# The last token group of the last projection: one sum formed in PSUM ahead of its product, two blocks stored by accumulation

## Chip, cores and metric

One core of one Trainium2 chip. The metric is the device time of one execution in microseconds (us), the median over several executions. "Span" is the length of the profiled execution, some 2 us shorter than the measured time. In the text PE is the matmul engine (TensorE), DVE is VectorE, ACT is ScalarE, POOL is GpSimd, SP is SyncE, which here only issues transfers. PSUM is the on-chip memory that the matmuls write to, SBUF the on-chip memory of all other tiles. A transfer lands when its completion is signalled; "landing" is the time from its issue to that.

## The reference, cut to what matters

The program normalizes x (2048 tokens x 1024), computes a windowed attention s with an output projection wo, and a gated MLP g on the same normalized x, and returns x + s * g. All arrays are bf16.

```python
xn = _layernorm(x, axis=-1)
s = _A_ref(xn, A_wqkv, A_wo)          # ends with  @ wo
g = _silu(_B_ref(xn, B_w1, B_w3, B_w2))
return x + s * g
```

The end of the kernel is the projection `@ wo` for the last group of 512 tokens, times g, plus x.

## The kernel before

The projection works on 2 x 2 blocks with seven products in place of eight (Strassen-Winograd). A token group gives four output blocks of 256 KB, named (u, dh): u selects the half of the tokens, dh the half of the columns. `finished` takes a block out of PSUM, multiplies by g and stores it. The code is cut; tile allocations are left out.

```python
def wo(b):                                    # b == 1, gp == 1 is the last group
    ...
    for gp in G2:
        last = b == 1 and gp == 1
        product(both(pa), gp, a11, b11, True)
        product(both(pe), gp, s1, t1, True)
        flush()                               # last product of the group before
        # pb gets a copy of pa (ACT); in the last group, two tiles and two half copies
        act_copy(sp5[:], pe[:])
        product(pbs, gp, s2, t2, False)
        # su2 gets a copy of pb (ACT); in the last group, two half copies
        product(both(pe), gp, s4, b22, False)
        finished(b, 0, 1, gp, pe, su2[:])     # pe + su2, a sum on DVE
        product(pbs, gp, s3, t3, False)
        finished(b, 1, 1, gp, pb, sp5[:])     # pb + sp5, a sum on DVE
        product(both(pa), gp, a12, b21, False)
        finished(b, 0, 0, gp, pa)
        # tail, run later: product(pbs, gp, a22, t4, False); finished(b, 1, 0, gp, pb)

def finished(b, u, dh, gp, ps, add=None):
    ...
    if b == 0 or gp == 0:                     # x lies in the output already
        to_bf16(d, ps, add)
        anchor["v"] = nc.vector.tensor_mul(g, d, g)
        nc.gpsimd.dma_start(out=rows_, in_=g, accum_op=ALU.add)
    elif (u, dh) != (1, 0):                   # last group: x is added on DVE
        to_bf16(d, ps, add)
        nc.vector.tensor_mul(g, d, g)
        nc.vector.tensor_add(g, g, xw[u, dh])
        nc.sync.dma_start(out=rows_, in_=g)
    else:
        # block (1, 0) in two halves, each with its own store on SP
        ...
```

So in all groups but the last the block is added to x inside the transfer: x was copied to the output long before (`residual`), and POOL issues an accumulating store. In the last group x comes in through `xw`, and SP issues plain stores.

Of the kernel before, what the change touches and what calls it, by code (L numbers as in the profile page):

```python
# [9 lines left out]
BF16 = mybir.dt.bfloat16  # L10
# [7 lines left out]
def kernel(  # L18
# [11 lines left out]
    nc = tc.nc  # L30
# [5 lines left out]
    CH = 512  # L36
# [9 lines left out]
    I = range(2)  # L46
    scale = float(Dh) ** -0.5
    hp = tc.high_priority

    x_flat = A_x.rearrange("b s d -> (b s) d")  # L50
# [32 lines left out]
        out=ident[:], in_=ident[:], compare_op=ALU.not_equal, fill=1.0,  # L83
# [5 lines left out]
        out=ones4[:], in_=ones4[:], compare_op=ALU.is_ge, fill=0.0,  # L89
# [3 lines left out]
        out=ones4[:], in_=ones4[:], compare_op=ALU.is_ge, fill=0.0,  # L93
# [5 lines left out]
        out=maskb[0:32], in_=maskb[0:32], compare_op=ALU.is_ge, fill=-1.0e9,  # L99
# [11 lines left out]
    pb = keep.tile([P, W, P], BF16, name="pb")  # L111
# [16 lines left out]
    def rows(f0, n, dt=BF16):  # L128
        v = h_sb[:, f0:f0 + n, :].rearrange("p f n -> p (f n)")
        return v if dt is BF16 else v.bitcast(dt)  # L130

    def bank2(name):
        return psum.tile([P, 2, CH], FP32, tag="mm", name=name)

    def k4(name, shape=(2, CH), dt=FP32):
        return kk.tile([P, *shape], dt, tag="k4", name=name)
# [10 lines left out]
    def mm(ps, lhs, rhs, first):  # L147
        n = len(lhs)
        for k in range(n):
            with behind("pe") if "open" in anchor else nullcontext():  # L150
                anchor["pe"] = nc.tensor.matmul(  # L151
                    ps, lhsT=lhs[k], rhs=rhs[k], start=(first and k == 0),
                    stop=(k == n - 1), skip_group_check=not first,
                )
# [4 lines left out]
    def act_copy(out_, in_):  # L159
        with hp():  # L160
            nc.scalar.copy(out=out_, in_=in_)  # L161
# [3 lines left out]
    def flush():  # L165
        while pend:
            pend.pop(0)()
# [59 lines left out]
    def behind(key):  # L227
        return tc.issue_after(anchor[key].ins) if key in anchor else nullcontext()
# [162 lines left out]
    def att_tile(shape, dt, name):  # L391
        return att.tile([P, *shape], dt, tag="a8", name=name)
# [109 lines left out]
    def run_hooks():  # L502
        while hooks:
            hooks.pop(0)()
# [43 lines left out]
    def bg(us):  # L548
        if us <= 0:
            return  # L550
        state_p[0] = tc.cur_priority
        pace["credit"] += us - pace["owed"]
        pace["owed"] = 0
        with priority(BG), behind("v"):
            while pace["credit"] > 0:
                t = next(att_it)
                if t is STOP:
                    pace["credit"] = min(pace["credit"], 6)
                    break
                else:  # L560
                    pace["credit"] -= t
# [23 lines left out]
    def release(key):  # L585
        free.extend(held.pop(key, []))
# [158 lines left out]
    def g_tile(b, u, dh, gp):  # L745
        f0 = {(0, 0): 10, (1, 1): 10, (0, 1): 6, (1, 0): 6}[u, dh] + 2 * gp
        col = {(0, 0): 0, (1, 1): CH, (0, 1): 0, (1, 0): CH}[u, dh]
        return h_sb[:, f0:f0 + 2, col:col + CH]
# [109 lines left out]
    wx = {}  # L858
# [23 lines left out]
    def wo(b):  # L882
        (a11, a12, a21, a22, s1, s2, s3, s4), (b11, b12, b21, b22, t1, t2, t3, t4) = wx[b]
        if b == 1:
            xt4 = att_tile((2, 2, 2, CH), BF16, "xw")
            for u in I:
                for dh in I:
                    xw[u, dh] = xt4[:, u, dh]
                    with behind("dl"):
                        nc.sync.dma_start(out=xw[u, dh], in_=out_rows(x_flat, 1, u, dh, 1))  # L890

        def product(ps, gp, lhs, rhs, first):
            for i in I:
                g = gp * 2 + i
                mm(ps[i], [lhs[:, j, g * P:(g + 1) * P] for j in range(4)], [rhs[:, j, :] for j in range(4)], first)

        both = lambda t: [t[:, i] for i in I]
        for gp in G2:
            run_hooks()
            last = b == 1 and gp == 1  # L900
            pa = bank2(f"wa{b}_{gp}")
            product(both(pa), gp, a11, b11, True)
            pe = bank2(f"we{b}_{gp}")
            product(both(pe), gp, s1, t1, True)
            flush()
            pb = [bank2(f"wb{b}_{gp}{i}")[:, i] for i in I] if last else bank2(f"wb{b}_{gp}")
            for i in I:
                if last:
                    act_copy(pb[i], pa[:, i])
            if not last:  # L910
                act_copy(pb[:], pa[:])
            pbs = pb if last else both(pb)
            sp5, su2 = k4(f"wsp{b}_{gp}"), k4(f"wsu{b}_{gp}")
            act_copy(sp5[:], pe[:])
            bg((7, 0)[gp] * (1 - b))
            product(pbs, gp, s2, t2, False)
            for i in I:
                if last:
                    act_copy(su2[:, i], pb[i])
            if not last:  # L920
                act_copy(su2[:], pb[:])
            product(both(pe), gp, s4, b22, False)
            finished(b, 0, 1, gp, pe, su2[:])
            product(pbs, gp, s3, t3, False)
            finished(b, 1, 1, gp, pb, sp5[:])
            product(both(pa), gp, a12, b21, False)
            finished(b, 0, 0, gp, pa)

            def tail(gp=gp, pb=pb, pbs=pbs):
                product(pbs, gp, a22, t4, False)  # L930
                finished(b, 1, 0, gp, pb)

            pend.append(tail)
        flush()
        release("wo")

    def out_rows(ap, b, u, dh, gp):
        g0 = ((2 * b + u) * NST + gp * 2) * P
        return ap[g0:g0 + 2 * P, dh * CH:(dh + 1) * CH].rearrange("(i p) n -> p i n", p=P)

    def to_bf16(d, ps, add):
        if add is None:
            nc.scalar.copy(out=d, in_=ps[:])
        elif isinstance(ps, list):
            for i in I:
                nc.vector.tensor_add(d[:, i], ps[i], add[:, i])
        else:
            nc.vector.tensor_add(d, ps[:], add)

    xw = {}  # L950

    copies = [((2 * b + u) * CH, CH // (1 + b), dh) for b in I for u, dh in ((0, 0), (1, 1), (0, 1), (1, 0))]

    def residual():
        if copies:
# [4 lines left out]
    def finished(b, u, dh, gp, ps, add=None):  # L960
        g = g_tile(b, u, dh, gp)
        n = {(0, 0): 0, (1, 1): 2, (0, 1): 4, (1, 0): 0}[u, dh] + gp
        d = h_sb[:, 16 + 2 * n:18 + 2 * n, CH:]
        rows_ = out_rows(out_flat, b, u, dh, gp)
        with hp():
            if b == 0 or gp == 0:
                to_bf16(d, ps, add)
                anchor["v"] = nc.vector.tensor_mul(g, d, g)
                nc.gpsimd.dma_start(out=rows_, in_=g, accum_op=ALU.add)
            elif (u, dh) != (1, 0):  # L970
                to_bf16(d, ps, add)
                nc.vector.tensor_mul(g, d, g)
                nc.vector.tensor_add(g, g, xw[u, dh])
                nc.sync.dma_start(out=rows_, in_=g)
            else:
                for i in I:
                    if i == 0:
                        nc.scalar.copy(out=d[:, i], in_=ps[i])
                    nc.vector.tensor_mul(g[:, i], ps[i] if i else d[:, i], g[:, i])
                    nc.vector.tensor_add(g[:, i], g[:, i], xw[u, dh][:, i])  # L980
                    nc.sync.dma_start(out=rows_[:, i], in_=g[:, i])


# [126 lines left out]
    b12 = rows(12, 2).rearrange("p (k n) -> p k n", k=KH)  # L1110
# [134 lines left out]
    with behind("dl"):  # L1245
        nc.sync.dma_start(out=xT[:], in_=x_dram[:])
        nc.sync.dma_start(out=xs[:], in_=xs_dram[:])
    wo(0)
    state.add("wo")
    mlp_up(1)  # L1250
    mlp_down(1, lambda: mid(1), (7, 10, 10, 9, 9, 3))
    wo(1)


# [28 lines left out]
```

## Time and profile before

| | before |
|---|---|
| time, median (first 3 runs) | 724.18 us (723.66 to 724.26) |
| span of the profile | 721.8 us |
| PE's last matmul ends | 715.89 |
| last DVE instruction ends | 718.69, 2.80 past PE |
| span ends | 5.91 past PE |

The prediction below shows the busy table, the chain and the end in order of time. Who waited for whom in the last 22 us (engine, line, waited for: us in total, times, longest us):

```profile
DVE h_sb L948 <- ACT wsu L161: 2.0, 1, 2.0
...
ACT wsu L161 <- PE wb L151: 1.1, 1, 1.1
```

and the same for the DMA queue of SP over the end. The closing wait of the program on its stores:

```profile
SPq L1278 <- DMA out_dram<-h_sb: 1.1, 3, 0.5
```

The view is what the change attacks: DVE idles 2.0 us for the copy wsu, and then runs behind PE to the end.

### The profile page before, as it was taken

The numbers are of one execution on the slowest core, as the hardware profiler recorded it, in microseconds if no ns is written. First come the engines' busy times: TensorE is split into PE (matmuls) and PEld (weight loads), VectorE is DVE, ScalarE is ACT, GpSimd is POOL, SyncE is SP. The second block draws the span as 40 slices with busy tenths as digits, with TensorE's granted clock in tenths as the row PEclk, the third lists the DMA queues.
The fourth block names the chain that finished last, engine by engine and source line by source line (L and its number), as shares of the span: only waits on it lengthen the run. The fifth ranks groups of instructions, "written<-read, shape, count | busy, mean of one in ns | idle before, by whom it ended". The sixth has DMA issues, their size and how long they took to land.

```text
span 721.8 us, 8746 instructions
## 1 busy us (share of the span) xinstructions
PE 710.0 (98%) x3313; PEld 346.2 (48%) x3367; DVE 624.9 (87%) x690; ACT 312.9 (43%) x326; POOL 95.7 (13%) x162
## 2 busy tenths in 40 slices
PE   8999999999999999999999999999999999999996
PEld 6655565654444444444444444444444444444442
DVE  7996879779879878978999999969859989999974
ACT  5745334356545456555555312034364573020233
POOL 0011100012300000233111000000435004000011
PEclk9999999999999999999999999999999999999999
DMA  9946257777754523558756547469799444563615
GB/s 337 275 125 182 82 185 228 258 249 238 246 172 153 191 71 117 173 191 268 246 174 216 190 132 250 144 205 385 168 276 336 139 138 150 168 202 129 199 36 108
DMA packets 119193, 139.51 MB, mean 193 GB/s; under 512 B 17648, under 2 KB 94448, under 8 KB 118512
## 3 DMA queue, kind: packets, MB, share of 16 engines
q1 hardware_dynamic: 104608, 97.01, 42.6%
q0 software_dynamic: 14544, 41.95, 18.0%
q8 instruction: 26, 0.43, 0.2%
q14 instruction: 15, 0.12, 0.1%
HBM read 96.21 MB, written 38.80 MB: 187 GB/s over the span
## 4 chain that ended last, share of the span: by engine, by line
PE 95%; ACT 2%; DVE 2%; issue 1%; DMA 0%; DVEq 0%; ACTq 0%
PE bm L151 20%; PE am L151 13%; PE em L151 13%; PE db L151 10%; PE bq L151 9%; PE de L151 7%; PE da L151 7%; PE eq L151 5%; PE aq L151 3%; PE wb L151 2%; PE af L151 2%; PE we L151 2%; PE wa L151 2%; DVE h_sb L236 1%; PE af L1049 1%
## 5 line engine op out<-in xcount | busy, mean ns | idle before, releaser
L151 PEld LDWEIGHTS <-wring 128*128 128x128 f16 (+1 forms) x1792 | 183.4, 102 | 204.3 <-issue 2.2
L151 PEld LDWEIGHTS <-h_sb 128*128 128x128 f16 (+1 forms) x1056 | 109.5, 104 | 118.4 <-issue 0.6
L151 PE MATMUL bm<-xs,wring 128*128 128x512 f16 x504 | 117.4, 379 | 0.2
L151 PE MATMUL am<-xT,wring 128*128 128x512 bf16 x322 | 79.0, 379 | 0.8
L151 PE MATMUL db<-wring,h_sb 128*128 128x512 f16 x336 | 73.2, 379 | 0.0
L481 DVE TENSOR_TENSOR BC<-Ep,vT 128x2048 bf16<-128x2048 bf16 x56 | 66.6, 1217 | 0.1
L426 DVE TENSOR_TENSOR pt<-qt,kT 128x4096 bf16<-128x4096 bf16 x24 | 54.9, 2290 | 0.6
L664 DVE TENSOR_TENSOR um<-em,um 128x1024 f32<-128x1024 f32 x28 | 34.2, 1222 | 21.0 <-PE em L151 13.3
L666 ACT ACTIVATE g<-um 128x1024 bf16<-128x1024 f32 x28 | 29.6, 1057 | 48.6 <-DVE um L664 48.6
L151 PE MATMUL da<-wring,h_sb 128*128 128x512 bf16 x219 | 48.7, 379 | 0.3
L467 POOL DMA_DIRECT2D Ep<-pb x64 | 38.0, 601 | 53.4 <-DVE pb L463 48.1
L151 PE MATMUL bm<-h_sb,wring 128*128 128x512 f16 x168 | 39.7, 379 | 0.0
L151 PE MATMUL em<-xs,wring 128*128 128x512 f16 x168 | 39.7, 379 | 0.0
L151 PE MATMUL em<-xT,wring 128*128 128x512 bf16 x161 | 39.2, 379 | 0.3
L491 DVE TENSOR_TENSOR oT<-oT,BC 128x2048 bf16<-128x2048 bf16 x32 | 39.0, 1219 | 0.3
L161 ACT COPY bm<-am 128x1024 f32<-128x1024 f32 x28 | 27.9, 998 | 25.9 <-PE am L151 25.9
L161 ACT COPY pm<-em 128x1024 f32<-128x1024 f32 x28 | 28.4, 1013 | 20.1 <-PE em L151 20.1
L161 ACT COPY um<-bm 128x1024 f32<-128x1024 f32 x28 | 28.4, 1014 | 18.9 <-PE bm L151 18.9
L685 ACT CAST g<-bm 128x1024 bf16<-128x1024 f32 x28 | 28.3, 1011 | 17.4 <-PE bm L151 17.4
L679 DVE TENSOR_TENSOR h_sb<-bm,pm 128x1024 bf16<-128x1024 f32 x21 | 25.6, 1218 | 5.1 <-PE bm L151 5.0
L489 DVE TENSOR_TENSOR BC<-BC 128x2048 bf16<-128x2048 bf16 x24 | 29.3, 1221 | 0.4
L428 DVE TENSOR_TENSOR pt<-pt 128x2048 bf16<-128x2048 bf16 x24 | 29.3, 1221 | 0.4
(197 smaller groups left out, 993.5 us busy)
## 6 DMA issues: line engine op xcount, KB each, us to landing
wring<-in_B_w_dram SPq DMA_DIRECT2D x61, 512.0 KB, 4.2
wring<-t_dram SPq DMA_DIRECT2D x16, 512.0 KB, 3.8
t_dram<-wring POOLq DMA_DIRECT2D x14, 512.0 KB, 3.8
wring<-t_dram SPq DMA_DIRECT2D x16, 384.0 KB, 4.9
wring<-in_B_w_dram SPq DMA_DIRECT2D x12, 384.0 KB, 4.5
wring<-in_A_x_dram SPq DMA_DIRECT2D x16, 256.0 KB, 4.2
Ep<-pb POOLq DMA_DIRECT2D x64, 64.0 KB, 4.9
wring<-in_A_wo_dram SPq DMA_DIRECT2D x8, 512.0 KB, 5.6
```

The lines of the kernel that those rows point to most:

```text
L151: anchor["pe"] = nc.tensor.matmul(ps, lhsT=lhs[k], rhs=rhs[k], start=(first and k == 0), stop=(k == n - 1), skip_group_check=not first,)
L161: nc.scalar.copy(out=out_, in_=in_)
L426: nc.vector.tensor_mul(p_t[:], q[:], kT[:, :, o:o + CH])
L428: nc.vector.tensor_add(p_t[:, 0:4, :], p_t[:, 0:4, :], p_t[:, 4:8, :])
L467: nc.gpsimd.dma_start(out=pr[c][r:P:NR, :, sq * P:(sq + 1) * P], in_=pb[sq * 32:(sq + 1) * 32, :, :])
L481: nc.vector.tensor_mul(dst, E[:, w, :].unsqueeze(1).to_broadcast([P, n, CH]), vT[:, js, o:o + CH])
L489: nc.vector.tensor_add(B, B, C)
L491: nc.vector.tensor_add(A, A, B if w0 else C)
L664: v = nc.vector.tensor_add(su2[:], pe[:], su2[:])
L666: nc.scalar.activation(out=hl["g"][:, :, CH:], in_=su2[:], func=ACTF.Silu)
L679: anchor["v"] = nc.vector.tensor_add(h[:, :, CH:], pb[:], sp5[:])
L685: nc.scalar.copy(out=hl["g"][:, :, 0:CH], in_=pb[:])
```

## The change

Intent: take a full-size sum off DVE's last stretch by forming it in PSUM before the last product is added there (pe = pb + sp5, where sp5 is a copy of pe, then pe += s4 * b22, so that ACT alone can take it out), and take two additions of x off DVE by letting the stores accumulate. Two smaller things come along: the product on block (0, 0) now reads PSUM on DVE, with no copy by ACT, and both halves of block (1, 0) are copied by ACT, where one was before. The diff, cut to its core (tile allocations, the loads of `xw` and the branch for block (1, 0) are left out, comments are added):

```diff
+    def wo_last(product, both):
+        product(both(pa), 1, a11, b11, True)
+        act_copy(pb[:], pa[:])
+        product(both(pe), 1, s1, t1, True)
+        act_copy(sp5[:], pe[:])
+        product(both(pb), 1, s2, t2, False)
+        with hp():
+            nc.vector.tensor_add(pe[:], pb[:], sp5[:])     # the sum, in PSUM
+        flush()                                            # 8 matmuls of the group before
+        product(both(pb), 1, s3, t3, False)
+        finished(1, 1, 1, 1, pb, sp5[:])
+        act_copy(pc[:, 1], pb[:, 1])
+        product(both(pe), 1, s4, b22, False)
+        finished(1, 0, 1, 1, pe)
+        product(both(pa), 1, a12, b21, False)
+        finished(1, 0, 0, 1, pa)
+        product([pb[:, 0], pc[:, 1]], 1, a22, t4, False)
+        finished(1, 1, 0, 1, [pb[:, 0], pc[:, 1]])
...
-    copies = [((2 * b + u) * CH, CH // (1 + b), dh) ...
+    copies = [((2 * b + u) * CH, CH if b == 0 or dh else CH // 2, dh) ...
...
-            if b == 0 or gp == 0:
+            if b == 0 or gp == 0 or dh == 1:
                 to_bf16(d, ps, add)
                 anchor["v"] = nc.vector.tensor_mul(g, d, g)
                 nc.gpsimd.dma_start(out=rows_, in_=g, accum_op=ALU.add)
-            elif (u, dh) != (1, 0):
-                to_bf16(d, ps, add)
-                nc.vector.tensor_mul(g, d, g)
-                nc.vector.tensor_add(g, g, xw[u, dh])
+            elif u == 0:
+                nc.vector.tensor_mul(g, ps[:], g)
+                nc.vector.tensor_add(g, g, xw[u])
                 nc.sync.dma_start(out=rows_, in_=g)
```

More of the change, by code (lines that the diff above doesn't have):

```diff
@@ L884, in wo @@
         if b == 1:
-            xt4 = att_tile((2, 2, 2, CH), BF16, "xw")
+            xt4 = att_tile((2, 2, CH), BF16, "xw")
             for u in I:
-                for dh in I:
-                    xw[u, dh] = xt4[:, u, dh]
-                    with behind("dl"):
-                        nc.sync.dma_start(out=xw[u, dh], in_=out_rows(x_flat, 1, u, dh, 1))
+                xw[u] = xt4[:, u]
+                with behind("dl"):
+                    nc.sync.dma_start(out=xw[u], in_=out_rows(x_flat, 1, u, 0, 1))
         def product(ps, gp, lhs, rhs, first):
@@ L899, in wo @@
             run_hooks()
-            last = b == 1 and gp == 1
+            if b == 1 and gp == 1:
+                wo_last(product, both)
+                break
             pa = bank2(f"wa{b}_{gp}")
@@ L905, in wo @@
             flush()
-            pb = [bank2(f"wb{b}_{gp}{i}")[:, i] for i in I] if last else bank2(f"wb{b}_{gp}")
-            for i in I:
-                if last:
-                    act_copy(pb[i], pa[:, i])
-            if not last:
-                act_copy(pb[:], pa[:])
-            pbs = pb if last else both(pb)
+            pb = bank2(f"wb{b}_{gp}")
+            act_copy(pb[:], pa[:])
+            pbs = both(pb)
             sp5, su2 = k4(f"wsp{b}_{gp}"), k4(f"wsu{b}_{gp}")
@@ L916, in wo @@
             product(pbs, gp, s2, t2, False)
-            for i in I:
-                if last:
-                    act_copy(su2[:, i], pb[i])
-            if not last:
-                act_copy(su2[:], pb[:])
+            act_copy(su2[:], pb[:])
             product(both(pe), gp, s4, b22, False)
@@ L935, in wo @@
         release("wo")
+    def wo_last(product, both):
+        (a11, a12, a21, a22, s1, s2, s3, s4), (b11, b12, b21, b22, t1, t2, t3, t4) = wx[1]
+        pa = bank2("va")
+        product(both(pa), 1, a11, b11, True)
+        pb = bank2("vb")
+        act_copy(pb[:], pa[:])
+        pe = bank2("ve")
+        product(both(pe), 1, s1, t1, True)
+        sp5 = k4("vsp")
+        act_copy(sp5[:], pe[:])
[5 more added lines that the diff above has]
+        finished(1, 1, 1, 1, pb, sp5[:])
+        pc = bank2("vc")
+        act_copy(pc[:, 1], pb[:, 1])
[3 more added lines that the diff above has]
+        finished(1, 0, 0, 1, pa)
+        ps = [pb[:, 0], pc[:, 1]]
+        product(ps, 1, a22, t4, False)
+        finished(1, 1, 0, 1, ps)
     def out_rows(ap, b, u, dh, gp):
@@ L943, in to_bf16 @@
             nc.scalar.copy(out=d, in_=ps[:])
-        elif isinstance(ps, list):
-            for i in I:
-                nc.vector.tensor_add(d[:, i], ps[i], add[:, i])
         else:
@@ L950 @@
     xw = {}
-    copies = [((2 * b + u) * CH, CH // (1 + b), dh) for b in I for u, dh in ((0, 0), (1, 1), (0, 1), (1, 0))]
+    blocks = ((0, 0), (1, 1), (0, 1), (1, 0))
+    copies = [((2 * b + u) * CH, CH if b == 0 or dh else CH // 2, dh) for b in I for u, dh in blocks]
     def residual():
@@ L976, in finished @@
                 for i in I:
-                    if i == 0:
-                        nc.scalar.copy(out=d[:, i], in_=ps[i])
-                    nc.vector.tensor_mul(g[:, i], ps[i] if i else d[:, i], g[:, i])
-                    nc.vector.tensor_add(g[:, i], g[:, i], xw[u, dh][:, i])
+                    nc.scalar.copy(out=d[:, i], in_=ps[i])
+                    nc.vector.tensor_mul(g[:, i], d[:, i], g[:, i])
+                    nc.vector.tensor_add(g[:, i], g[:, i], xw[u][:, i])
                     nc.sync.dma_start(out=rows_[:, i], in_=g[:, i])
```

## The prediction

> **What bounds the kernel now.** I read the page's busy table first, then the waits of TensorE (PE), then the chain of waits, the instructions in order of time and the DMA answer for the last 13 us, because the change touches only the end and one early copy.
>
> The page, part 1 (busy us, share of the span, instructions):
>
> ```profile
> PE 710.0 (98%) x3313; PEld 346.2 (48%) x3367; DVE 624.9 (87%) x690; ACT 312.9 (43%) x326; POOL 95.7 (13%) x162
> ```
>
> PE is busy 710.0 of 721.8 us. Its waits for other engines' work add up to 2.5 us (1.3 + 0.7 + 0.5), all in the opening. So nothing that moves under PE work counts; what remains is what PE does not cover: the opening, and the end after the last matmul. The change deletes no product, so a gain can only come from the end.
>
> The chain that ended last, by start, length and what (the pieces after 709 us):
>
> ```profile
> 709.33 0.96 PE wb L151 x4
> ...
> 710.32 0.59 ACT wsu L161
> ...
> 710.93 1.23 DVE h_sb L948
> 712.16 0.35 DVE h_sb L946
> ...
> 712.67 0.68 DVE h_sb L972
> 713.35 0.60 DVE h_sb L946
> ...
> 714.47 0.70 DVE h_sb L972
> ...
> 715.19 0.69 DVE h_sb L973
> ...
> 716.40 0.68 DVE h_sb L979
> ...
> 717.60 0.42 DVE h_sb L979
> 718.02 0.34 DVE h_sb L980
> ```
>
> Here the chain leaves PE 5.6 us before PE's own end and runs on VectorE (DVE). DVE starts its first sum of the last group at 710.93, held by ACT's second half copy into wsu, and then has no pause. The instructions in order of time show the rest:
>
> ```profile
> 709.24 1.18 POOL L969 DMA_DIRECT2D out_dram<-h_sb  x1 [4.00 <-DVE h_sb L968]
> ...
> 714.00 1.89 PE L151 MATMUL wb<-wring,oT 128*128 128x512 f16 x8
> ...
> 714.58 3.50 SPq L974 DMA_DIRECT2D out_dram<-h_sb  x3
> ...
> 717.94 0.75 DVE L980 TENSOR_TENSOR h_sb<-h_sb,xw 128x512 bf16<-128x512 bf16 x2
> 718.42 0.84 SPq L981 DMA_DIRECT2D out_dram<-h_sb  x2
> ```
>
> PE's last product ends at 714.00 + 1.89 = 715.89, DVE ends at 717.94 + 0.75 = 718.69, the last store is issued at about 718.85, and the span ends at 721.8. So the end is 2.80 us of DVE backlog past PE, then 3.1 us of store landing and closing.
>
> The DMA answer for 709 to 722 us (40 slices of 0.325 us; KB each, us from issue to landing):
>
> ```profile
> GB/s 0 0 0 0 0 0 50 85 192 189 192 95 3 0 0 0 0 0 0 9 350 391 57 0 328 381 98 0 0 135 381 388 303 290 117 0 0 0 0 0
> ...
> out_dram<-h_sb SPq DMA_DIRECT2D x3, 256.0 KB, 2.2
> out_dram<-h_sb POOLq DMA_DIRECT2D x1, 256.0 KB, 4.1
> out_dram<-h_sb SPq DMA_DIRECT2D x2, 128.0 KB, 1.8
> ```
>
> The accumulating store issued by POOL at 709.24 moves data in slices 6 to 12, 710.95 to 713.2: 2.2 us for 256 KB, starting 1.7 us after its issue. The plain stores reach 380 to 390 GB/s, about 0.7 us for 256 KB, starting 0.9 us after issue. The last data of the kernel move at about 720.4.
>
> **What the Trainium skill says.** "VectorE: DVE Perf Modes", section "The perf-mode tier table", says that a tensor_tensor on 16-bit SBUF operands runs at 2x and at 1x with any PSUM operand. The trace agrees: 1.23 us for 1024 elements from PSUM against 0.69 us when all is bf16 in SBUF. So the PSUM-to-PSUM sum is estimated at the same 1.22 to 1.23 us; no row of this trace writes PSUM from DVE.
> "DMA: Bandwidth & Descriptors", section "SWDGE vs HWDGE vs iDMA", says that accumulation during a DMA goes through GpSimd only; the trace has it on POOL, landing in 4.1 us against 2.2. The same page, section "Issuing engines are not separate DMA queues", says that all issuers share the same 16 engines. In the kernel before the two kinds do not overlap in the end, so no number here shows what it costs; it is my main doubt.
> "PSUM — Partial Sum Buffer", section "PSUM bank collisions raise a hardware error", says that two engines must not touch one bank at once, two readers included. This explains why in the new instruction order ACT's copy into vc waits for DVE, which reads the same vb. The kernel before has no such pair at the end to check it by.
>
> **The change part by part.**
>
> *TensorE.* Both orders have 6736 PE rows and the same products. The wa run starts at 700.10 and its first eight matmuls belong to the old group, at 1.89 us for eight with 0.38 for the last, so 0.216 us apart: the last group starts at 700.10 + 1.73 = 701.83. From there 56 matmuls of the last group and 8 left over from the old one make 64 x 0.216 = 13.82, plus 0.16 for the longer last one: 715.81. The trace has 715.89, so PE stalls by 0.08 us only. The new order is va, one matmul of the old group, ve, vb (s2), seven of the old group, vb (s3), ve (s4), va (a12), vb/vc (a22). The one new wait is vb (s3) behind the DVE sum into ve. Step by step: vb (s2) ends at 707.40; the seven old matmuls fill PE up to 708.75; the DVE sum starts at 707.43 (its other input, vsp, is ready at 706.71) and ends at 707.43 + 1.22 = 708.65. It is hidden by 0.1 us. PE then ends at about 715.83, as before.
>
> *ACT.* Removed: two 0.59 us wsu copies, split copies into wb. Added: a 1.01 us cast of ve, one 0.57 us copy to vc. ACT is 43% busy, so only its waits matter: vb (s3) ends 710.64, DVE reads it 710.67 to 711.90, the vc copy runs 711.93 to 712.50 and the ve cast 712.53 to 713.54. The last product needs vc at 714.80; no PE stall.
>
> *DVE.* Before, after 710.9: 1.23 + 0.68 + 0.69 (sums), 3 x 0.69 (products), 3 x 0.69 (xw sums), 0.68 + 0.42 (halves), 2 x 0.42 (xw halves) = 8.7 us nominal, 7.76 us with neighbours overlapping. After: the s3 sum 1.22 and its product 0.69 (to 712.59), the product on ve 0.69 (713.57 to 714.26), the product directly from va in PSUM 1.22 (from 714.14, va being ready at 714.10, to 715.36), its xw sum 0.69 (to 716.08), then four halves of 0.42: product 716.00 to 716.42, sum to 716.85, product 716.77 to 717.19, sum to 717.62. ACT's casts of the halves end at 715.59 and 716.45, so DVE waits for neither. DVE ends at 717.62 in place of 718.69: 1.07 us earlier. This is the whole direct gain: one full-size sum moved ahead of PE's last 5 us, two xw sums gone (taken over by DMA accumulation).
>
> *DMA.* Two 256 KB blocks go by accumulation on POOL and two xw loads of 256 KB go; two early copies of x to the output grow from 256 to 512 KB. The early ones sit at 187 to 236 us, where PE is busy 9.95 of each 10 us and the DMA share is 0.4 to 1.0: worth nothing, I expect. At the end POOL now issues at 710.70 (the old group's last block, 1.46 us later than before because its product waits behind vb), 712.62 and 714.29. With 1.7 us to first data and 2.2 us of data each, back to back: 712.4 to 714.6, to 716.8, to 719.0. The plain stores are issued at 716.11, 716.88 and 717.65, with data from 717.0 on. If they were alone, the last lands at 717.65 + 1.8 = 719.45, against 718.85 + 1.8 = 720.65 before: gain 1.2 us. If they share engines with the third accumulation without any overlap, the work after 717.0 is 2.0 + 0.7 + 0.7 = 3.4 us, and data end at 720.4, as before: gain 0. The truth should lie between, since packets of two queues overlap in part. I choose two thirds of the gain: 0.8 us.
>
> Sum: 724.18 - 0.8 = 723.4.
>
> **The rivals.**
> 1. *The accumulations take over the end.* For it: three in a row after 710.7, the slowest kind of store, the last issued only 3.4 us before DVE ends; its alone-landing, 714.29 + 4.1 to 5.2 = 718.4 to 719.5, is near 719.45. Against: it starts before the stores, and a busy share over 1 shows overlapping packets. Time: 724.0 to 724.4.
> 2. *PE stalls on the sum in PSUM.* For it: slack of 0.1 us only, and a DVE write into PSUM is not in this trace. Against: same element count and rate as other PSUM rows. Even 0.3 us more moves PE's end by 0.2. Time: 723.6.
> 3. *The gain is full*, if the engines serve plain stores quickly beside accumulation. Time: 723.0. Beyond that a floor stands: PE's end 715.83, an ACT cast 0.6, two halves 0.84, about 3.1 to the end gives 720.4 of span, or 722.8.
> 4. *The larger early copies delay weight loads and stall PE.* Against: loads are issued far ahead of use, and PE waits for no DMA anywhere. Time: 724.5.
>
> **Range and chances.** The change can touch only the last 5.9 us after PE, 0.8% of the time; for 2% it would have to save or cost 14.5 us. So within 2% is nearly sure: 0.98, with 0.01 on each side for a disturbance of the early schedule. The range runs from the full gain with some luck, 722.6, to no gain, 724.3; the runs of before spread by 0.6 us.
>
> **What would show it.** Right: no wsu tile in the last group, PE's last matmul within 0.2 us of 715.9, DVE ending near 717.6 with the chain through va, and the last store's data ending 0.4 to 1.2 us earlier. Wrong: a PE gap before the vb (s3) product; the chain ending in an accumulation that lands after the plain stores; stores of 128 KB taking over 2.5 us to land; PE gaps between 187 and 245 us.

## The result, and the profile after

The changed kernel took 724.95 us (median of 4 runs, 724.49 to 725.65) against 724.05 us before. The ratio is 1.0014, 95% interval 0.9997 to 1.0031. Ratios in this text are the mean time of one kernel's fast runs over that of the other's of the same rounds, so not quite the ratio of the medians quoted. By the 2% mark that is as forecast, but the time lies above the predicted range of 722.6 to 724.3, and the predicted small gain became at best nothing.

The end of the changed kernel in order of time (start, us, engine, line, operation):

```profile
707.80 1.23 DVE L942 TENSOR_TENSOR ve<-vb,vsp 128x1024 f32<-128x1024 f32 x1 [3.73 <-PE vb L151]
...
709.09 1.39 PEld L151 LDWEIGHTS <-oT 128*128 128x128 f16 x7 [0.16 <-issue]
...
711.27 1.18 POOL L986 DMA_DIRECT2D out_dram<-h_sb  x1 [5.73 <-DVE h_sb L985]
...
713.26 1.17 POOL L986 DMA_DIRECT2D out_dram<-h_sb  x1 [0.81 <-DVE h_sb L985]
...
714.84 1.18 POOL L986 DMA_DIRECT2D out_dram<-h_sb  x1 [0.41 <-DVE h_sb L985]
715.12 1.03 PE L151 MATMUL vc<-wring,oT 128*128 128x512 f16 x4
...
716.44 0.38 SPq L990 DMA_DIRECT2D out_dram<-h_sb  x1
...
717.27 1.10 SPq L996 DMA_DIRECT2D out_dram<-h_sb  x2
717.58 0.42 DVE L995 TENSOR_TENSOR h_sb<-h_sb,xw 128x512 bf16<-128x512 bf16 x1
```

The first line is the sum in PSUM: 1.23 us, as estimated. PE hardly notices it: the weight load at 709.09 starts 0.16 us late, which the view puts down to no other engine (`issue`). PE ends at 715.12 + 1.03 = 716.15, DVE at 718.00. DVE is thus 1.85 us behind PE in place of 2.80: this part of the change works. The three POOL lines are the accumulating stores, the last issued 1.6 us before the first plain store at 716.44.

The DMA answer of the changed kernel for 709 to 722.4 us (40 slices of 0.335 us; in the line DMA each digit is the busy share of the 16 DMA engines in tenths, 9 being 90% or more; KB each, us to landing):

```profile
DMA  0000000000009999969999994128999999720000
GB/s 3 0 0 0 0 0 0 0 0 0 0 0 70 119 141 196 180 89 61 147 177 196 159 95 6 9 34 144 193 205 251 342 385 373 254 83 6 0 0 0
...
out_dram<-h_sb POOLq DMA_DIRECT2D x3, 256.0 KB, 4.3
out_dram<-h_sb SPq DMA_DIRECT2D x1, 256.0 KB, 4.5
out_dram<-h_sb SPq DMA_DIRECT2D x2, 128.0 KB, 3.7
```

and the closing wait of SP:

```profile
SPq L1293 <- DMA out_dram<-h_sb: 2.7, 4, 1.8
```

In the kernel before, plain stores landed 2.2 and 1.8 us after issue; here 4.5 and 3.7. Three humps of at most 205 GB/s are the accumulations (slices 12 to 29), and only then comes the run at 340 to 385 GB/s that marks plain stores. The first plain store is issued at 716.44. The DMA answers for 716 to 719 and for 719 to 719.5 us count what moved of POOL's queue (q0) and of SP's (q1): packets, MB, share of 16 engines:

```profile
q0 software_dynamic: 350, 0.34, 108.8%
q1 hardware_dynamic: 3, 0.00, 0.3%
...
q0 software_dynamic: 62, 0.05, 69.0%
q1 hardware_dynamic: 79, 0.08, 47.0%
```

So until 719.0 only three packets of SP's queue move, and then both queues for about half a us. SP's closing wait grows from 1.1 to 2.7 us.

Where the 0.6 us between the two profiles go:

| stretch, us | before | after | difference |
|---|---|---|---|
| start of the last group's first product (before: as worked out in the prediction) | 701.83 | 702.13 | +0.30 |
| from there to PE's end | 14.06 | 14.02 | -0.04 |
| PE's end to DVE's end | 2.80 | 1.85 | -0.95 |
| DVE's end to the span's end | 3.11 | 4.40 | +1.29 |
| span | 721.8 | 722.4 | +0.6 |

The first row is not the change's: over all kernels run here, most with the same program up to there, the last projection starts between 691.47 and 692.76 us, and the profile of before is the earliest of all. The 0.30 us are there long before anything that was changed: a copy by ACT at 99.22 us in the profile of before starts at 99.52 in that of the changed kernel, and at 99.52 in that of copies_only below. The last two rows are the matter: the gain on DVE is given back, and more, in the landing of the stores.

### The profile page after: what moved, and what is told of

It is laid out like the page before. It is cut to its first block, busy times and chain, and to the rows that moved or that the text cites. A ratio compares the mean times of both kernels' runs of the same rounds, so it can differ in the third digit from the quotient of the medians.

```text
span 722.4 us, 8791 instructions
## 1 busy us (share of the span) xinstructions
PE 712.3 (99%) x3367; PEld 346.1 (48%) x3367; DVE 624.3 (86%) x687; ACT 312.8 (43%) x325; POOL 98.0 (14%) x164
## 4 chain that ended last, share of the span: by engine, by line
PE 90%; DVE 4%; DMA 3%; ACT 2%; issue 1%; SPq 1%; DVEq 0%; ACTq 0%
PE bm L151 20%; PE am L151 13%; PE em L151 13%; PE bq L151 9%; PE db L151 8%; PE da L151 7%; PE de L151 7%; PE eq L151 5%; PE aq L151 3%; PE wb L151 2%; DVE h_sb L236 1%; PE wa L151 1%; PE we L151 1%; DMA wring<-in_A_wo_dram 1%; DMA wring<-in_A_wqkv_dram 1%
## 5 line engine op out<-in xcount | busy, mean ns | idle before, releaser
L986 POOL DMA_DIRECT2D out_dram<-h_sb x14 | 17.4, 1451 | 96.5 <-DVE h_sb L985 96.4
```

## The experiments

Theory A: the accumulating stores occupy the DMA engines that all queues share, and the last plain stores get through only when they are done. Rivals: B, any transfer from POOL's queue does this, accumulating or not; C, the loss comes from outside the last group, above all from the larger early copies; D, both kinds of store work on the same rows of memory; E, the hold is in SP's own queue. Further, that the sum in PSUM costs. Theory A holds two things: that the plain stores come late because of the accumulating ones, which the runs test, and how, by occupied engines, which they test only in part.

The 14 kernels from after_again on ran in 5 paired rounds each (4 to 6 runs). "Past PE" is from the end of PE's last matmul in the profile, which takes out the varying opening; the views give the span to 0.1 us, so the last column is good to about 0.05. Each kernel has one profile, the changed one two. Where a kernel is wrong it is said; with three of the four the comparison with the reference did not notice: it passed even not_stored, which leaves out s * g in two blocks of sixteen. So "correct" below says little about the s * g of single blocks. The diffs are cut: the loads of `xw` and the sizes of the early copies follow the blocks that are stored plainly.

| kernel | time, median | ratio to before | DVE ends past PE | span ends past PE |
|---|---|---|---|---|
| before (first profile) | 724.05 | | 2.80 | 5.91 |
| changed | 724.95 | 1.0014 | 1.85 | 6.25 |
| after_again | 724.73 | 1.0009 | 1.85 | 6.13 |
| plain_on_pool (wrong) | 723.35 | 0.9985 | 1.85 | 4.56 |
| not_stored (wrong) | 723.41 | 0.9989 | 1.84 | 4.50 |
| half_acc (wrong) | 723.03 | 0.9984 | 1.84 | 4.82 |
| acc_elsewhere (wrong) | 725.40 | 1.0015 | 1.84 | 6.93 |
| stores_on_act | 724.74 | 1.0008 | 1.84 | 6.58 |
| copies_only | 723.96 | 0.9996 | 2.80 | 5.92 |
| acc_only | 725.07 | 1.0015 | 2.44 | 6.58 |
| acc_01_only | 723.49 | 0.9994 | 1.85 | 5.53 |
| acc_11_only | 722.97 | 0.9986 | 2.31 | 5.40 |
| sum_only | 723.22 | 0.9988 | 2.31 | 5.22 |
| sum_pool_add | 724.98 | 1.0016 | 3.94 | 6.87 |
| acc_11_cast | 722.75 | 0.9982 | 2.10 | 5.14 |
| sum_cast | 722.91 | 0.9982 | 2.11 | 4.94 |

The intervals of the ratios are about 0.0013 wide to each side (0.0017 for the changed kernel). The column "past PE" is the sharper tool for causes; the ratio decides what is faster.

**after_again**, the changed kernel unedited.

> The changed kernel again, as the measure for the others. In its first profile PE's last matmul ended at 716.15, DVE 1.85 us later, the span 6.25 us later (before: 2.80 and 5.9), and the plain stores landed 3.5 to 4.5 us after issue (before 1.8 to 2.3). Theory A, the accumulating stores hold up the last plain stores on the shared DMA engines: the same again, DVE about 1.9 us and the end about 6.2 us past PE, ratio to before 1.0003 to 1.001. Rival C, the loss comes from outside the last group (opening loads 0.3 us later, larger early copies): the end past PE is within 0.1 us of before's 5.9 and the loss is in when PE's last matmul ends.

Ratio 1.0009, 6.13 us past PE, landing 3.3 us and more. The larger part of theory A's expectation holds and C's fails: the end past PE is not that of before.

**plain_on_pool** (wrong result).

```diff
-                nc.gpsimd.dma_start(out=rows_, in_=g, accum_op=ALU.add)
+                last = b == 1 and gp == 1
+                nc.gpsimd.dma_start(out=rows_, in_=g, **({} if last else {"accum_op": ALU.add}))
```

> Wrong result on purpose: the two blocks go out on the same POOL queue at the same moments, but as plain overwrites without the addition. Theory A, it is the read-add-write of the accumulation that occupies the engines: the two transfers take about 0.7 us of data each in place of 2.2, the last plain stores land in 1.8 to 2.6 us, the end is 5.0 to 5.4 us past PE, ratio 0.9985 to 0.9995. Rival B, any transfer from POOL's software queue holds back the plain stores: landing stays 3.5 to 4.5 us, the end 6.2 us past PE, ratio as the changed kernel. Rival C: no difference from the changed kernel.

```profile
out_dram<-h_sb POOLq DMA_DIRECT2D x3, 256.0 KB, 2.9
out_dram<-h_sb SPq DMA_DIRECT2D x1, 256.0 KB, 2.2
out_dram<-h_sb SPq DMA_DIRECT2D x2, 128.0 KB, 1.7
```

This is the DMA answer of that kernel for its last 13 us. The same bytes leave by the same queue at the same moments, and the plain stores land in 2.2 and 1.7 us, as before the change. The end is 4.56 us past PE, even less than expected. It is the addition inside the transfer, not POOL's queue: B falls as the cause of this loss. What a plain transfer of POOL's does that is still under way when SP's stores come, the run does not show: here POOL's bytes are through by 717.8 and SP's first ones move after 718.3.

**not_stored** (wrong result).

```diff
-                nc.gpsimd.dma_start(out=rows_, in_=g, accum_op=ALU.add)
+                if not (b == 1 and gp == 1):
+                    nc.gpsimd.dma_start(out=rows_, in_=g, accum_op=ALU.add)
```

> Wrong result on purpose: the two blocks are computed but not stored at all. Theory A and rival B both: landing 1.8 to 2.3 us, the end 1.85 + 3.1 = 4.95 us past PE, ratio about 0.9985 to 0.999: the gain predicted without the accumulations. Rival C: the end past PE stays near 5.9 and the ratio at or over 1.0003.

4.50 us past PE, 0.45 less than expected: without the two transfers the end is 1.6 to 1.75 us earlier than with them, and 1.4 us earlier than in the kernel before.

**half_acc** (wrong result).

```diff
-                nc.gpsimd.dma_start(out=rows_, in_=g, accum_op=ALU.add)
+                h = 1 if (b, u, dh, gp) == (1, 0, 1, 1) else 2
+                nc.gpsimd.dma_start(out=rows_[:, 0:h], in_=g[:, 0:h], accum_op=ALU.add)
```

> Wrong result on purpose: the changed kernel, but the last accumulation (block (0,1), issued near 714.8) moves only one of its two halves, 128 KB in place of 256; the other half is not stored. If the plain stores are served only after the accumulated bytes are through, one after the other, half of 2.2 us goes: landing 2.4 to 3.4 us in place of 3.3 to 4.5, the end 5.0 to 5.4 us past PE in place of 6.1 to 6.25, ratio 0.9990 to 1.0002. If a fixed cost of any accumulation in flight holds the stores: the end stays within 0.3 us of 6.2.

```profile
out_dram<-h_sb SPq DMA_DIRECT2D x1, 256.0 KB, 3.0
out_dram<-h_sb SPq DMA_DIRECT2D x2, 128.0 KB, 2.2
out_dram<-h_sb POOLq DMA_DIRECT2D x1, 128.0 KB, 3.8
```

The DMA answer for its end: 128 KB less to accumulate, and the plain stores land 1.5 us sooner (4.5 to 3.0, 3.7 to 2.2); the end comes 1.3 to 1.4 us earlier than in the changed kernel, and at 4.82 and 0.9984 it is better than expected. Half of an accumulation's 2.2 us would be 1.1. So a fixed cost of any accumulation falls, and the hold grows with the bytes that are still to be accumulated when the plain stores come, here by at least their own time. It does not grow with all accumulated bytes: the 384 KB that are left of the two blocks cost only 0.3 us (4.82 against 4.50 in not_stored).

**acc_elsewhere** (wrong result).

```diff
-                nc.gpsimd.dma_start(out=rows_, in_=g, accum_op=ALU.add)
+                to = h_dram[u][:, :, 0:CH] if b == 1 and gp == 1 else rows_
+                nc.gpsimd.dma_start(out=to, in_=g, accum_op=ALU.add)
```

> Wrong result on purpose: the changed kernel with its two last accumulations made into an unused piece of scratch memory, same size, same moments, 1 KB runs, in place of the output rows whose other halves the plain stores write. Theory A (the read-add-write occupies the engines whatever its destination): as the changed kernel, landing 3.3 to 4.5 us, the end 6.0 to 6.3 us past PE, ratio 1.0005 to 1.0015. Rival D, the hold comes from both kinds of store working on the same rows of memory: landing 1.7 to 2.6 us, the end 4.5 to 5.2 us past PE, ratio 0.9985 to 0.9995.

6.93 us past PE, landing over 4 us: worse still, so D falls. That it is worse than the changed kernel by 0.7 us was not expected; these two accumulations land in 5.5 us (median) in place of 4.8. Why the scratch memory is slower was not pursued.

**stores_on_act**: the last two plain stores from ACT's queue.

```diff
-                    nc.sync.dma_start(out=rows_[:, i], in_=g[:, i])
+                for i in I:
+                    nc.scalar.dma_start(out=rows_[:, i], in_=g[:, i])
```

> Correct result: the changed kernel with the last two plain stores (128 KB each) issued from ACT's queue in place of SP's; the first one of 256 KB stays on SP. Theory A (the hold is in the shared engines): landing of the two stays over 3 us, the end 5.9 to 6.3 us past PE, ratio as the changed kernel. Rival E (the hold is in SP's own queue, behind its first held store): the two land in under 2.6 us and the end is set by the 256 KB store, near 5.6 us past PE.

```profile
out_dram<-h_sb SPq DMA_DIRECT2D x1, 256.0 KB, 4.7
out_dram<-h_sb ACTq DMA_DIRECT2D x2, 128.0 KB, 4.0
```

From another queue they land as late (4.0 us): E falls. The end, 6.58 us past PE, is a little over the expected 6.3.

**copies_only**: the kernel before with the larger early copies alone.

```diff
-    copies = [((2 * b + u) * CH, CH // (1 + b), dh) for b in I for u, dh in ((0, 0), (1, 1), (0, 1), (1, 0))]
+    blocks = ((0, 0), (1, 1), (0, 1), (1, 0))
+    copies = [((2 * b + u) * CH, CH if b == 0 or dh else CH // 2, dh) for b in I for u, dh in blocks]
```

> Correct result: the kernel before with nothing changed but the two early copies of x to the output grown from 256 to 512 KB (the rows are overwritten later, so this is idle work). If they are hidden, as I hold: the end as before (DVE 2.8 us, span 5.9 us past PE), ratio 0.9997 to 1.0003. Rival C, they delay weight loads or later traffic: PE ends 0.3 us or more later and the ratio is 1.0004 to 1.0012.

Ratio 0.9996 and an end past PE as before (2.80 and 5.92): the early copies are hidden, and C's main candidate falls, within the interval of 0.9982 to 1.0010. In its profile PE does end 0.29 us later than in that of before (716.18), but that shift is there at 99 us already, and the larger copies are issued from 211 us on.

**acc_only**: the kernel before with the storage part alone, its order and sums kept.

```diff
-            if b == 0 or gp == 0:
+            if b == 0 or gp == 0 or dh == 1:
```

> Correct result: the kernel before with only the storage part of the change (its sums, its order and its separate wb tiles kept; the two blocks accumulated on POOL, larger early copies). The two accumulations should be issued near 713.4 and 714.7 and move data until about 719.5. Theory A (the accumulation's read-add-write occupies the shared engines): DVE ends about 2.0 to 2.2 us past PE in place of 2.80, the plain stores land in 3 to 4 us in place of 1.8 to 2.3, the end is 6.0 to 6.5 us past PE, no better than 5.9, ratio 0.9998 to 1.001. Rival: only the chain of three accumulations in a row, as the change has it, holds the stores: the end 5.0 to 5.4 us past PE, ratio 0.999 or less.

6.58 us past PE, ratio 1.0015, interval 1.0003 to 1.0028: the storage part alone makes the kernel slower, by a little more than expected. DVE gains less than expected (2.44, not 2.0 to 2.2). It takes no chain of three back to back: here the earlier accumulation is issued at 709.67, over 4 us ahead of the other two.

**sum_only**: the changed kernel with both blocks stored plainly.

```diff
+            plain = b == 1 and gp == 1 and dh == 1
+            if plain:
+                to_bf16(d, ps, add)
+                nc.vector.tensor_mul(g, d, g)
+                nc.vector.tensor_add(g, g, xw[u, dh])
+                nc.sync.dma_start(out=rows_, in_=g)
```

> Correct result: the sum in PSUM kept, the two blocks added to x on DVE and stored plainly as before, early copies as before. DVE takes back two additions of 0.69 us, estimated DVE end 2.4 us past PE. Theory A: landing 1.8 to 2.3 us, the end 5.4 to 5.6 us past PE, ratio 0.9993 to 0.9998: faster than both kernels. Rival that the sum in PSUM is what costs (a PE stall): PE ends 0.2 us or more later than 715.9 relative to its start of the last group and the ratio is over 1.0.

723.22 us, ratio 0.9988: faster than the changed kernel, and about 0.9 us under before (interval 0.9976 to 1.0001, so just short of certain); the end, 5.22 us past PE, is better than expected. The sum in PSUM, with the new order around it, is the good half of the change. DVE pays 0.46 us for the two additions (2.31 against 1.85), and the accumulation cost more than that.

**acc_01_only** and **acc_11_only**: the same test with only one of the two blocks plain.

> Correct result: the sum in PSUM, block (1,1) stored plainly (issued near 713.6), block (0,1) alone accumulated (issued near 714.8, as the second of the end in place of the third). Theory A with the engines serving in order of arrival: its data run from about 716.6 to 718.7, the plain stores issued at 716.4 to 718.0 are held in part and land in 2.4 to 3.6 us, the end 5.2 to 5.8 us past PE. If only a queue of accumulations hurts: landing 1.7 to 2.3 us, the end 4.5 to 4.7 us past PE.

> Correct result: the sum in PSUM, block (1,1) accumulated (issued near 713.3, data over by 717.2), block (0,1) added on DVE and stored plainly. Theory A: the accumulation is over before the last plain stores start, so they land in 1.7 to 2.4 us; DVE ends 2.3 us past PE as in the kernel with the sum only; the end 5.1 to 5.4 us past PE, ratio 0.9985 to 0.9995. If any accumulation in the last 10 us costs: landing over 3 us and the end over 5.8 us past PE.

With block (0,1) accumulated, issued at 714.66, the plain stores issued after it land in 2.4 to 3.4 us and the end is 5.53 past PE, as theory A said for a part of the hold. With block (1,1) accumulated, issued at 713.11, the last three stores land in 1.7 to 2.3 us and the end is 5.40. So an accumulation costs little if its bytes are through before the last plain stores start (from DVE's end to the span's end 3.09 us, against 2.91 in sum_only), and more when it comes later (3.68).

**sum_pool_add**: an attempt at a faster kernel, with POOL adding x.

```diff
-                nc.vector.tensor_add(g, g, xw[u, dh])
+                nc.gpsimd.tensor_add(g, g, xw[u, dh])
```

> Correct result, an attempt at a faster kernel: as the one with the sum only, but POOL adds x to the two blocks, in place of DVE or of the accumulating DMA. The addition's time on POOL is in no trace so far; if it is under 2 us, DVE ends 1.85 us past PE, all stores are plain and land in 1.7 to 2.4 us, the end is 4.5 to 4.9 us past PE, ratio 0.998 to 0.9988: the fastest. If POOL's additions slow DVE down or take over 3 us, DVE rows of 0.69 and 0.42 us grow, or block (0,1) is the last to land, and the end is 5.2 us past PE or later.

```profile
712.98 2.12 POOL L988 TENSOR_TENSOR h_sb<-h_sb,xw 128x1024 bf16<-128x1024 bf16 x1 [0.65 <-PE ve L151]
713.73 1.92 DVE L987 TENSOR_TENSOR h_sb<-h_sb 128x1024 bf16<-128x1024 bf16 x1 [0.90 <-ACT h_sb L963]
...
715.72 2.12 POOL L988 TENSOR_TENSOR h_sb<-h_sb,xw 128x1024 bf16<-128x1024 bf16 x1 [0.63 <-DVE h_sb L987]
...
716.81 1.58 DVE L996 TENSOR_TENSOR h_sb<-h_sb,xw 128x1024 bf16<-128x1024 bf16 x1
```

A miss, and by the named risk: in order of time, DVE instructions that start during POOL's addition take 1.92 and 1.58 us in place of 0.69, and both end 0.55 us after POOL's does (POOL's at 715.10 and 717.84). This is what the Trainium skill, "SBUF — State Buffer", section "Who interferes with whom", states: a DVE instruction with two SBUF inputs contends with a GpSimd instruction that reads SBUF, and the later one waits. The trace agrees, with these numbers.

**acc_11_cast** and **sum_cast**: the two good kernels, with the product on va taken from a bf16 copy by ACT.

```diff
-                nc.vector.tensor_mul(g, ps[:], g)
+                d = h_sb[:, 16:18, CH:]
+                nc.scalar.copy(out=d, in_=ps[:])
+                nc.vector.tensor_mul(g, d, g)
```

> Correct result, an attempt at the best of both: the sum in PSUM, only block (1,1) accumulated, and the product on va from a bf16 copy by ACT (1.0 us on ACT, then 0.69 us on DVE) in place of 1.22 us on DVE from PSUM. DVE was the last engine and 0.5 us of it goes, 0.3 us is given back by waiting for ACT: DVE ends 2.0 to 2.1 us past PE, the end 5.0 to 5.2 us past PE, ratio 0.9982 to 0.9992, 0.1 to 0.3 us under the kernel with (1,1) accumulated and no cast.

> Correct result: the sum in PSUM, no block accumulated, the product on va from ACT's bf16 copy. Same DVE end as with (1,1) accumulated, since its additional 0.69 us lie where DVE waits for ACT's cast of ve: 2.0 to 2.1 us past PE, the end 5.0 to 5.2 us past PE, ratio 0.9982 to 0.9992, within 0.2 us of the one with (1,1) accumulated.

```profile
714.37 1.01 ACT L996 CAST h_sb<-va 128x1024 bf16<-128x1024 f32 x1 [0.64 <-PE va L151]
...
715.42 0.69 DVE L997 TENSOR_TENSOR h_sb<-h_sb 128x1024 bf16<-128x1024 bf16 x1 [0.24 <-ACT h_sb L996]
```

In sum_cast's order of time, ACT has the copy ready while DVE is still on another block; DVE idles 0.24 us for it and is done with this product 0.05 us after PE's end (716.11); in sum_only the product straight from PSUM is done 0.26 us after it (716.44). Both kernels have ratio 0.9982 (interval 0.9970 to 0.9995, clear of 1 for both), medians 722.75 and 722.91 against 724.01 us. They beat both given kernels by more than 1 us. Which of the two is better is not resolved.

## Why the prediction was wrong, by its own steps

- **What bounds the kernel; only the end counts.** Right: copies_only changes nothing, the shift of the opening is there at 99 us already, and no part of the difference that I could attribute to the change lies before the last group.
- **TensorE.** Right: the sum took 1.23 us (estimated 1.22 to 1.23) and PE needed 14.02 us for the last group in place of 14.06. Rival 2, a PE stall, did not happen.
- **ACT.** Right in its waits: the copy into vc waited for DVE as foreseen and did not hold PE. That the rule on PSUM banks is the reason for that wait, no run shows.
- **DVE.** Right: predicted 1.07 us nearer to PE's end (1.79 us by its steps), measured 0.95 (1.85).
- **DMA, early part.** Right (copies_only, 0.9996).
- **DMA, at the end: the step that failed.** The prediction put the accumulations at three in a row of 2.2 us each, which the trace bears out (first data near 713.0, last near 719.5). It then wrote that with no overlap between the two kinds of store the gain is 0, that "The truth should lie between, since packets of two queues overlap in part", and chose 0.8 us of 1.2. The overlap is what it had wrong. Measured, there is next to none: from 716 to 719 three packets of SP's queue move beside 350 of POOL's, and the plain stores begin at about 719.0, 2.5 us after issue instead of 0.9. From DVE's end to the span's end it took 4.40 us in place of 3.11, a term of +1.29 where about +0.3 was implied (1.07 on DVE less 0.8). Without the two accumulations it takes only 2.66 (not_stored), so they cost 1.6 to 1.75 us. half_acc shows how: 128 KB less accumulation, 1.3 to 1.4 us less end. The lower bound of "gain 0" was itself too kind, by 0.2 to 0.3 us; part of that may be that POOL's issues came 0.25 us later relative to PE's end than worked out (711.27 is 4.88 before PE's end, against 5.13).
- **The rivals.** Rival 1, the accumulations take over the end, is what happened; its own reason against ("it starts before the stores, and a busy share over 1 shows overlapping packets") was the error: in before's last 22 us the share passes 1 where POOL's queue alone moves (1.15 from 704 to 705, and 1.09 from 711 to 712 with a single store), so it says nothing of plain stores beside accumulating ones.
- **Range.** The upper end, 724.3, stood for "no gain". The measured loss at the end in the profiles is 0.2 to 0.35 us, which from 724.05 gives about 724.3; the medians, 724.95 and 724.73, are 0.4 to 0.6 us beyond that. I can't attribute that rest: it lies inside the intervals of the ratios (down to 0.9997), and the varying opening is of that size.

What stays open: why the engines serve plain stores so late. The packets show that they come after the accumulated ones, and also a pause of about 0.7 us near 717.5 in the first profile in which little moves for either; in the second profile of the same kernel the pause is a slow stretch instead. In it the engines stand almost idle (digits 1 and 2 of the line DMA), and the first plain store, due at about 717.35 by the 0.9 us of before, still does not start. So busy engines are not the whole reason why it waits; what the engines do in the pause no view shows, and how the hold comes about is not shown.

## What to carry to other kernels

A store that adds to memory was cheap only where nothing behind it was urgent: 256 KB of it took 2.2 us of nearly all engines against 0.7 plain, and later plain stores landed about that much later. Near the end of a kernel count the landing of the last store, not the end of the last engine, and give up an accumulation there for a 0.69 us addition. When a change has two halves, run each alone: here the new order with the sum in PSUM gained 0.9 us and the accumulated stores alone lost 1.1 us.

## What the Trainium skill lacked or had wrong

- "DMA: Bandwidth & Descriptors", section "Issuing engines are not separate DMA queues": it says that transfers of all issuers run on the same 16 engines and interleave. The runs agree on the shared engines, but plain stores behind accumulating ones landed in 3.5 to 4.5 us in place of 1.8 to 2.3; nothing in that section warns that interleaving may amount to waiting (3 packets of SP's queue beside 350 of POOL's from 716 to 719 us).
- The same page, section "SDMA does more than copy", names the addition without a rate. The runs: 256 KB accumulated in bf16 in about 2.2 us of data (peak 205 GB/s), plain in about 0.7 us (peak near 390 GB/s), landing 4.1 to 5.3 us against 1.7 to 2.3.
- "VectorE: DVE Perf Modes", section "The perf-mode tier table", speaks of PSUM operands, but gives no duration for a sum that writes PSUM. The runs: an fp32 sum of PSUM and SBUF into PSUM, 1024 elements, takes 1.23 us, against 1.22 to 1.23 into SBUF as bf16.
- "ScalarE: Activation LUTs", section "Step-by-step: what each stage is for", says that ScalarE writes PSUM faster than SBUF. For copies of 1024 fp32 elements out of PSUM the rows show 1.00 us into PSUM (vb), 1.01 into SBUF as fp32 (vsp) and 1.02 as bf16 (ve's cast): next to nothing.
